# New written orders, buffers and warming places for a four-layer spectral kernel on one core

## The chip, the core and the metric

The kernel runs on one core of a Trainium2 chip. A core has a matrix engine (TensorE, PE in the profile, with PEld for its loading of weights), three engines that work on rows of up to 128 partitions (VectorE or DVE, ScalarE or ACT, GpSimd or POOL), and SyncE (SP), which here only issues transfers. The metric is the time of one execution on the device in microseconds (us).

## The reference

A sequence x of 2048 positions with 512 channels passes through four residual layers, A, B, A and B. A multiplies a two-dimensional spectrum by weights. B is a convolution along the sequence with a kernel K of its own for every channel, which is itself to be computed from the parameters; both B layers use the same K.

```python
def A(x):                                     # x: 1 x 2048 x 512
    return irfft2(rfft2(x) * (w_r + 1j * w_i), s=(2048, 512))

def B(u):                                     # 512 channels, 128 modes each
    dt = exp(log_dt)
    a = -exp(log_A_real) + 1j * A_imag
    C = (C_real + 1j * C_imag) * dt[:, None]
    P = exp((a * dt[:, None])[:, :, None] * arange(2048))
    K = 2.0 * einsum("dn,dnl->dl", C, P).real
    y = irfft(rfft(u.T, 4096) * rfft(K, 4096), 4096)[:, :2048]
    return y.T + u * D_skip

x = x + A(layernorm(x)); x = x + B(layernorm(x))
x = x + A(layernorm(x)); x = x + B(layernorm(x))
```

## The kernel before

**The work.** All Fourier transforms are matrix products with constant tables. The sequence is cut into 16 parts of 128 positions, so that a transform of 2048 is a pass over the 128 (products) and a pass over the 16 (products again, after a rearrangement). Data are tiles of 128 partitions by 512 numbers in f32.

- layer_a loads rows of x (`u`, line 428, on SP's queue; the table `ta` and the edge weights `ew` as well), takes layer-norm statistics (L359 to L382 on DVE), folds the rows (`spread`, L462 to L473), multiplies by tables on PE (halves, L330, and side_by_side, L336), by the spectral weights (L542 to L549 on DVE and POOL), and goes back.
- kernel_parts and kernel_time build K: exponentials and sines on ACT (L832), terms `qp` on DVE (L886, L888), products `pk` and their copies `kw` (L864), sums over the modes `pv` (L899), stored by way of `stage` (L907). kernel_constants (L812, L813) loads the tables `kb` and `ni` on POOL's queue; end_weights (L392 to L402) loads `ew` and prepares the end columns on POOL (L399).
- layer_b takes u's transform by row products into PSUM, copies them to `z` with ACT (L663), transposes z in 32 by 32 blocks on DVE (L669), multiplies by K's spectrum `kk` (`wb`, L991), adds (L1003, mostly POOL), transforms back (ACT copies in L1011 and L1015) and adds the residual (`za`, `xw`, L1029).

While the first A runs, K is computed; kernel_freq (K's spectrum) and the first B follow, with the rest of K between. Then come the second A and the second B, with nothing beside them. In the profiled execution the stages overlap. Roughly, the first A and most of K fill the first 300 us, the first B with the rest of K lies up to about 500, the second A up to about 613, and the second B, the last stage, from 613 to the end.

**The orders.** net_kernel emits all instructions in the order of the program. Then take_turns goes over each of the five engines: `TURNS[engine]` lists the engine's instructions by their number in emission, in the order in which they shall stand in the engine's stream. A list holds, for instance, 5046 numbers for PE. Each engine executes its own list strictly as a queue, except that waits between engines come from the data: an instruction waits until what it reads is written, and until the buffer that it writes is free. A transfer is issued by an instruction in a list too (mostly SP's), and the 16 DMA engines carry it out later.

**The buffers.** A phase is a group of pools in SBUF or PSUM, each with a tag, a size and a number of buffers ("rooms"). `ROOMS` says for each tile of a tag, in turn, which room it gets (room, L287).

**The pads.** Net.ps makes a tile in PSUM. `WARM` gives, for the number of a tile, how many pads are emitted ahead of its first product: a pad is one call of halves, two passes of 128x128 numbers of a constant tile `warm` against itself, written into the new tile and overwritten after. They keep PE busy where it would wait.

PE takes most products in two halves of 64 columns: halves emits one pass for each, with the output in the lower or upper 64 partitions of the PSUM tile; `128*64` in a row of the profile is such a half.

Of the kernel before, what the change touches and what calls it, by code (L numbers as in the profile page):

```python
# [10 lines left out]
F32 = mybir.dt.float32  # L11
# [27 lines left out]
WT = 4  # L39
WA = 7  # L40
# [16 lines left out]
MAG = 4  # L57
# [195 lines left out]
class Net:  # L253
# [870 lines left out]
def net_kernel(ctx, tc, x, w, ends, kin, log_dt, d_skip, out, **cst):  # L1124
# [19 lines left out]
    with ExitStack() as outer:  # L1144
        with ExitStack() as early:
            early.enter_context(net.phase("pk", P, pk=(2048, PK), pv=(2048, PV)))
            with net.phase("p", P, p1=(2048, 8 - PK - PV), p2="p1", p3="p1"), \
                    net.phase("a", x=(32768, 1), ta=(8192, 1), ca=(6912, 1), u=(16384, 2), w=(2056, WA), wt=(2056, WT),
# [4 lines left out]
                with net.phase("v", val=(10240, 1), hp=(HP, 2)):  # L1153
# [5 lines left out]
                    early.enter_context(net.phase("k", side="right", kw=(1024, 2), mag=(6144, MAG),  # L1159
# [10 lines left out]
            outer.enter_context(net.phase("b", t2=(8192, 1), u=(16384, 2), kk=(2048, 8), ta="t2", wt="w", wb="w", xw="w"))  # L1170
# [64 lines left out]
222-225 242-249 256-259 226-231 260 264-266 250 267 251 261 232 268-272 252 262 273 253 263 233 274-279 298-307  # L1235
280-281 254 312 282 286 255 313 287 314 288 315 289 283-285 308-311 316-321 290-291 322-331 338-339 292-295
340-342 346-349 343-345 296-297 350-351 332-335 366-371 358-365 336-337 374-387 414-417 372-373 402-413 418-423
464-465 424-427 388-393 448-451 466-467 452-455 476-483 512-513 456-461 514-515 394-397 516-517 398-401 462-463
428-431 518-519 432-433 520-523 434 436-437 435 438-439 352-357 548-551 554-557 524-525 468-475 552-553 440-441
484-487 558 492-494 504 495 559 505-507 488-491 442-447 496-497 526-533 498-499 508-511 500-503 534-543 560-561  # L1240
544-547 562-564 568 580 569 581 570 582 571 583 565-567 606-609 572-573 586-593 574-577 584 594 578 612 579 595
613 585 610 596-597 611 614-617 620-621 618-619 598-599 626-627 600-601 622-623 628 634-635 629-630 636-637
631-633 654-657 602-605 638-639 660-667 624-625 640-643 658 668-670 688 671 689 659 690-691 646-651 672-673
652-653 644-645 674-677 694-701 678 702-704 692 705 693 679 738-741 706-711 680-685 752-757 712 760 758 761 759
713 742-743 686 762-763 687 764-771 798-800 808-809 801-807 810-811 772-773 812 834-837 813-815 714-721 774-775
784-785 816-819 838-839 786-787 722-729 788-791 840-843 792-795 730-737 844-845 796-797 820-823 826-831 854-857
878 900-902 832-833 744-749 858-863 750-751 910 824-825 846-849 776-777 850-851 778-783 942 903 852-853 904-906
879-880 886-887 864-875 888 881-884 907-908 943-944 894-896 889-890 945 876-877 946-948 885 909 897 911-912
891-893 926-936 949 898 937-938 913-914 939 915-917 899 970-973 940-941 918-925 974-975 962-969 950-961 976-983
# [298 lines left out]
```

## Time and profile before

| | |
|---|---|
| time, three runs | 716.2, 717.33 and 723.59 us, median 717.33 |
| profiled execution | span 713.4 us; the page gives no other time of its own for it |
| instructions | 23503 |
| busy PE, DVE, ACT, POOL | 626.0, 601.9, 438.2, 357.3 us |
| moved by DMA | 81.32 MB, mean 114 GB/s |

The span is the time from the first to the last instruction of the profiled execution; a time of a run holds some microseconds around it. In a table of windows each row is one stretch in us from the span's start. It gives the busy time of each engine with its number of instructions, the granted clock of PE as a share of full speed (PEclk), and the mean busy share and rate of the DMA engines. A group row gives the line, engine, operation and tiles (written <- read), the number of instructions, their busy sum in us, the mean length of one in ns, and the idle time just before them with what ended it. A timeline row gives the start, the length, and in brackets the idle time before and who ended it.

### The profile page before, as it was taken

The page shows a single profiled execution, that of the slowest core. Times are in us where ns is not written, and L with a number is a line of the kernel's source. Part 1 is how long each engine was busy: PE and PEld are TensorE (multiplying, and loading weights), DVE is VectorE, ACT ScalarE, POOL GpSimd, SP SyncE. Part 2 cuts the span into 40 slices and gives each one's busy share as a digit, 9 for nine tenths or more (in the row PEclk, how much of TensorE's full clock was granted, in tenths as well). Part 3 has the DMA queues.
Part 4 walks back from the last instruction along what each step waited for, and adds up shares of the span by engine and source line. Part 5 has one row for each costly group of instructions (what it writes and reads, how often), then busy time and mean ns, then how long its engine had stood idle before and what let it go on. Part 6 is the DMA issues. An engine that isn't in the chain of part 4 may idle for free. (4 is left out here: it accounts for less than half of the span.)

```text
span 713.4 us, 23503 instructions
## 1 busy us (share of the span) xinstructions
PE 626.0 (88%) x9580; PEld 491.3 (69%) x9580; DVE 601.9 (84%) x1348; ACT 438.2 (61%) x946; POOL 357.3 (50%) x565
## 2 busy tenths in 40 slices
PE   4459989989996999889999997984989899999996
PEld 3237867878674867667858876774877766577876
DVE  4998497998999799969999676869588699799993
ACT  3558999997664796778868524333767427333322
POOL 1533528672852704543196356452056484286870
PEclk9779999999999999999999999997999999999999
DMA  8602611613558350455544689222123103335514
GB/s 282 229 0 89 210 48 47 122 62 43 167 133 245 107 138 32 65 128 94 163 62 136 195 198 246 80 106 75 61 77 89 46 2 104 125 103 149 156 34 111
DMA packets 137355, 81.32 MB, mean 114 GB/s; under 512 B 70976, under 2 KB 116928, under 8 KB 136352
## 3 DMA queue, kind: packets, MB, share of 16 engines
q1 hardware_dynamic: 136992, 79.30, 40.1%
q8 instruction: 76, 1.25, 0.7%
q0 software_dynamic: 256, 0.52, 0.4%
q14 instruction: 31, 0.25, 0.1%
HBM read 54.90 MB, written 25.43 MB: 113 GB/s over the span
## 5 line engine op out<-in xcount | busy, mean ns | idle before, releaser
L1003 POOL TENSOR_TENSOR u<-wb,wb 64x512 f32<-64x512 f32 x90 | 123.2, 1373 | 66.0 <-DVE wb L991 60.9
L336 PE MATMUL p<-z,mb 128*64 128x512 f32 (+2 forms) x480 | 108.0, 517 | 1.7 <-DVE wb L991 1.3
L899 PE MATMUL pv<-qp 128*64 128x128 f32 x1024 | 81.6, 279 | 5.0 <-ACT stage L907 4.2
L991 DVE TENSOR_TENSOR wb<-p,kk 128x512 f32<-128x512 f32 x128 | 81.5, 676 | 4.3 <-POOL u L1003 2.3
L336 PEld LDWEIGHTS p<-mb,u 128*64 128x64 f32 x2048 | 73.1, 138 | 13.1 <-issue 6.7
L336 PE MATMUL p<-mb,u 128*64 128x64 f32 x2048 | 74.3, 223 | 4.4 <-issue 2.0
L663 ACT COPY z<-p 128x512 f32<-128x512 f32 x96 | 52.4, 595 | 41.8 <-PE p L336 31.6
L669 DVE STREAM_TRANSPOSE z<-z 128x512 f32<-128x512 f32 x96 | 59.3, 675 | 19.8 <-ACT z L663 19.7
L899 PEld LDWEIGHTS pv<-qp 128*64 128x64 f32 x1024 | 64.4, 139 | 15.8 <-ACT stage L907 6.9
L1113 POOL TENSOR_SCALAR w<-w,norms 128x128 f32<-128x128 f32 x64 | 34.7, 554 | 67.7 <-DMA w<-h 29.8
L547 POOL TENSOR_TENSOR w<-w,w 64x257 f32<-64x257 f32 x48 | 34.7, 724 | 66.8 <-DVE w L542 45.3
L1015 ACT COPY u<-p 128x512 f32<-128x512 f32 x64 | 35.9, 590 | 48.7 <-PE p L336 45.3
L330 PE MATMUL p<-w,w 128*64 128x256 f32 x256 | 38.2, 438 | 27.8 <-DVE w L463 11.6
L330 PE MATMUL pk<-kb,th 96*64 96x256 bf16 (+1 forms) x384 | 56.5, 312 | 1.5 <-DVE qp L888 1.1
L542 DVE TENSOR_TENSOR w<-wt,p 128x514 f32<-128x514 f32 x64 | 42.7, 688 | 17.1 <-PE p L336 9.6
L864 DVE TENSOR_SCALAR kw<-pk 128x512 bf16<-128x512 f32 x64 | 42.9, 680 | 16.5 <-PE pk L330 16.1
L330 PE MATMUL p<-warm 128*64 128x128 f32 x612 | 49.2, 284 | 3.2 <-DVE half L1139 1.1
L336 PE MATMUL p<-t,w 64*64 64x128 f32 x1024 | 42.1, 280 | 10.2 <-DMA w<-kt 3.5
L336 PEld LDWEIGHTS p<-z,mb 128*64 128x64 f32 x480 | 39.7, 137 | 16.1 <-issue 7.9
L330 PEld LDWEIGHTS p<-w,w 128*64 128x64 f32 x256 | 24.7, 156 | 36.3 <-DVE w L463 12.7
L336 PE MATMUL p<-w,ca 128*64 128x257 f32 x256 | 45.0, 385 | 4.1 <-ACT w L526 1.5
L832 ACT ACTIVATE kf<-pk 128x512 f32<-128x512 f32 x64 | 38.8, 606 | 15.4 <-PE pk L330 13.8
(179 smaller groups left out, 1617.1 us busy)
## 6 DMA issues: line engine op xcount, KB each, us to landing
wt<-in_w SPq DMA_DIRECT2D x32, 257.0 KB, 2.7
kf<-kk SPq DMA_DIRECT2D x32, 256.0 KB, 3.3
kk<-kf SPq DMA_DIRECT2D x32, 256.0 KB, 2.7
u<-in_x SPq DMA_DIRECT2D x16, 256.0 KB, 6.8
hr<-in_x SPq DMA_DIRECT2D x16, 256.0 KB, 3.9
kt<-stage SPq DMA_DIRECT2D x32, 128.0 KB, 5.2
h<-hr SPq DMA_DIRECT2D x16, 256.0 KB, 3.0
w<-kt SPq DMA_DIRECT2D x32, 128.0 KB, 3.1
```

Source lines behind the costliest of these rows:

```text
L330: self.nc.tensor.matmul(out[64 * r:64 * r + 64], weights[:, 64 * r:64 * r + 64], data, **k)
L336: last = self.nc.tensor.matmul(out, weights, data, start=not more, stop=True, skip_group_check=True).ins
L542: nc.vector.tensor_mul(m[pl], W, px[:, None, :].to_broadcast([128, 2, 257]))
L547: e[0].tensor_sub(Y[0:64, v], m[0][hs, 0], m[1][hs, 1])
L663: nc.scalar.copy(tiles["z"][:, :, :, b, m:m + 2].rearrange("p u j m r -> p (u j) (m r)"), ps[b].rearrange("p u j m r -> p (u j) (m r)"))
L669: nc.vector.transpose(tiles["zt"][:, u:u + 8].rearrange("p u j d -> p (u j d)"), tiles["z"][:, u:u + 8].rearrange("p u j b m r -> p (u j b ...
L832: nc.scalar.activation(*a, **k)
L864: nc.vector.tensor_scalar(whole, p, MAGIC, -MAGIC, op0=ALU.add, op1=ALU.add)
L899: nc.tensor.matmul(p[64 * t:64 * t + 64, g], QP[:, c, 2, d:d + 2].rearrange("p s a -> p (s a)"), QP[:, c, 0:2, d:d + 2].rearrange("p k s b ...
L991: nc.vector.tensor_mul(split(m[c, pl], "du", [32, 16]), by_channel(p), split(k[c], "du", [32, 16]))
L1003: self.added = e[0].tensor_sub(y[0:64], v[0, 0], v[1, 1]), e[1].tensor_add(y[64:128], v[0, 1], v[1, 0])
L1015: nc.scalar.copy(V[:, :, j, :, d:d + 8].rearrange("p n q d -> p q n d"), p.rearrange("p (q n) d -> p q n d", q=2))
```

## The change

All instructions of real work stay as they are. Four things change.

1. phase() now also allocates every room of a tag at once when the phase opens, in a fixed order, and three phases (a, k and b) name their tags in another order. So tiles come to lie at other addresses.
2. The lists of TURNS are new for all five engines. PE's list has 4892 entries instead of 5046, by the pads; those of DVE (1348), ACT (922), POOL (561) and SP (316) are as long as before. Numbers in PE's list are those of emission with the pads counted, so the old and the new numbers of the same product differ.
3. WARM is new: 154 pads at 87 tiles instead of 231 at 92.
4. ROOMS is new: which room each tile gets.

Some moves that can be read from the lists: SP's rows of u come in the order 0, 1, 2, 3 instead of 0, 2, 1, 5, and the load of `ew` is ninth; POOL's issues of ni and kb are its 12th and 13th instruction instead of the first two, behind the first of end_weights (L399); ACT's early square root of one number (L1202, `root`) goes from first to about fifteenth.

The diff, with the lists cut to their first lines:

```diff
@@ -280,6 +280,11 @@
         with self.tc.tile_pool(name=name, bufs=1, space=space, side=side, reuse_waits="tile") as pool:
             for tag, v in tags.items():
                 self.tags[tag] = self.tags[v] if isinstance(v, str) else (pool, name, tag, *v)
+            for tag, v in tags.items():
+                if not isinstance(v, str):
+                    for k in range(v[1]):
+                        room = f"{tag}{k}" if v[1] > 1 else tag
+                        pool.tile([128, v[0] // 4], F32, tag=room, bufs=1, name=f"{name}_{room}")
             yield
         for tag in tags:
             del self.tags[tag]
...
@@ -1145,7 +1150,7 @@
         with ExitStack() as early:
             early.enter_context(net.phase("pk", P, pk=(2048, PK), pv=(2048, PV)))
             with net.phase("p", P, p1=(2048, 8 - PK - PV), p2="p1", p3="p1"), \
-                    net.phase("a", x=(32768, 1), ta=(8192, 1), ca=(6912, 1), u=(16384, 2), w=(2056, WA), wt=(2056, WT),
+                    net.phase("a", x=(32768, 1), u=(16384, 2), ta=(8192, 1), w=(2056, WA), ca=(6912, 1), wt=(2056, WT),
                               wv="w", junk="w"):
                 A = net.layer_a(w, src=xv, dst=hd)
                 early.enter_context(net.phase("k0", side="right", kb=(5120, 1), ni=(256, 1), th=(1536, TH)))
...
@@ -1156,7 +1161,7 @@
                         interleave(A[0][:PC])
                         interleave(A[0][PC:], made[:LATE])
                     net.end_weights(ends)
-                    early.enter_context(net.phase("k", side="right", kw=(1024, 2), mag=(6144, MAG),
+                    early.enter_context(net.phase("k", side="right", mag=(6144, MAG), kw=(1024, 2),
                                                   qp=(6144, QP), kf=(2048, KF), stage=(8192, 1)))
                     K, marks = net.kernel_time(parts, kt, list(range(32)), GROUP)
                     K = ahead(tc, K, KP)
...
@@ -1167,7 +1172,7 @@
                 with net.phase("e", hr=(2048, 8)):
                     interleave(K[cuts[0]:cuts[1]], A[2])
             outer.enter_context(net.phase("f", t=(16384, 1), z=(16384, 2), w=(2056, WB)))
-            outer.enter_context(net.phase("b", t2=(8192, 1), u=(16384, 2), kk=(2048, 8), ta="t2", wt="w", wb="w", xw="w"))
+            outer.enter_context(net.phase("b", kk=(2048, 8), t2=(8192, 1), u=(16384, 2), ta="t2", wt="w", wb="w", xw="w"))
             pm = [int(c) for c in PM.split(",")]
             early.enter_context(net.phase("pm", P, p1=(2048, pm[0]), p2=(2048, pm[1]) if pm[1] else "p1",
                                           p3=(2048, pm[2]) if pm[2] else "p1"))
...
     "tensor": """
-0-17 23-24 18-19 25-28 20-21 32-39 22 29-31 40-65 67-70 76-79 66 80-81 71-72 82-83 73-75 85-88 94-95 84 89-92
-103-106 93 96-97 112-113 107-108 98-101 109-110 102 114-115 111 116-119 121-124 120 125-126 130-131 127-128
-132-133 129 134-161 172-179 163-168 180-181 169-171 182-193 162 194-211 218-219 234-235 212-217 220-221 236-241
...
+0-1 9-10 18-27 11-16 2-5 28-29 17 6-7 30-31 8 32-33 35-38 34 39-65 76-77 67-68 66 69-74 78-81 75 82-83 85-88 84
+89-90 94-95 91-92 96-97 93 103-104 112-115 98-99 105-106 100-102 107-111 116-119 121-124 130-131 120 125-128
+132-135 129 136-153 157-158 154-155 168-169 156 170-171 159-160 166-167 161-162 172-173 176-177 163-165 178-189
+206-213 174-175 190-191 266-273 224-231 194-197 200-203 192-193 214 198-199 215-217 232 204-205 233-235 218-221
...
     "vector": """
-2 1 0 3-5 19 6 20 7 21 8 22 9 23 10-12 24 13-14 16-17 25 15 26 18 27-28 65 29 35 37 30 52 36 54 38 55 66 31 53
-39 41 76 101 40 78 32 77 42 79 43 59 67 80 82 119 81 83 121 123 60 125 84 44 72 85 102 68 61 73-74 33 75 86 34
...
+2 0 14 3 5 17 4 19 6 20 7 12 21 18 8 22 15 23 9 16 1 10 24 11 25 28 13 26 65 32 35 27 29 53 52 30 54 66 55 59 37
+39 36 101 38 41 76 40 42 78 43 48 80 77 82 60 119 31 72-73 79 121 81 67 44 122-123 83-84 61 68 125 120 85 126
+124 33 74 45 86 75 34 46 93 62 87 47 94 50 56 98 57 99 49 100 58 103 138 51 127 102 128 104 63 105 88-89 91 129
...
     "scalar": """
-611 0 9 1 5 2 6 23 10 24 11 14 34 15 3-4 7-8 12-13 29 50 18 51 40 39 49 16-17 19-20 25-26 52 30-31 35-36 64 62
...
+0 9 5 1 23-24 34 10-11 6 2 29 7 50 611 14 8 3 15 12 18 51 40 4 39 16 25 17 19 30 20 31 52 26 64 35-36 21-22 63
+62 61 13 41 27 42 32 28 49 33 45 53 57 54 37-38 58 46 73 43 69 44 78 70 65 47-48 66 83 55-56 98 59 79 74 60 67
...
     "gpsimd": """
-0-2 4 3 6 5 8 7 44-46 55 60 67 13 74 10 9 16-23 12 11 15 14 25 24 27 26 29 28 31 30 33 32 35 34 37 36 39 38 41
...
+3 5 10 2 6 8 7 9 44 4 45 1 0 24 46 14 11 13 15 25 12 16-19 28 20-21 67 22 74 32 27 30 33 29 23 26 60 31 54 35 34
+36 53 37 40 38 55 41 39 42 59 43 47-50 58 51 56 52 57 62-63 65 61 73 66 72 64 68 70 69 81 71 75 79 88 76-77 80
...
     "sync": """
-0 4 1 10 5 2 6 9 7 13 18 14 17 12 16 27 31 15 34 11 109 35 106 8 30 38 19 105 20 3 22 21 24 23 25-26 32-33
...
+0-1 4-5 7 2 6 9 27 12 10 13 11 17-18 8 15 30 16 14 19 31 20 35 38 34 105 3 22 21 106 23-24 26 25 28 33 29 32 37
+109 36 40-41 68 66 86 83 39 77 70 74 72 42 44 43 45 50-51 55 52 48 46 53 49 47 54 58 64 57 56 63 65 76 62 60 59
...
-WARM = {22: 7, 35: 3, 55: 1, 104: 3, 116: 2, 120: 5, 123: 6, 146: 2, 158: 1, 160: 2,
-        165: 2, 175: 3, 201: 1, 205: 2, 210: 2, 214: 2, 240: 2, 272: 1, 355: 1, 386: 1,
-        400: 1, 410: 1, 413: 1, 415: 4, 428: 1, 440: 5, 459: 1, 552: 3, 573: 3, 583: 1,
-        586: 1, 636: 1, 639: 3, 643: 2, 650: 2, 652: 7, 655: 4, 656: 3, 670: 1, 674: 1,
-        680: 5, 690: 3, 692: 2, 693: 1, 704: 1, 706: 3, 711: 1, 726: 1, 732: 1, 735: 3,
-        742: 1, 754: 5, 759: 3, 777: 1, 779: 2, 783: 2, 789: 4, 791: 1, 797: 3, 807: 1,
-        809: 1, 814: 3, 834: 1, 867: 1, 963: 3, 972: 4, 992: 1, 1007: 3, 1014: 6, 1017: 3,
-        1035: 1, 1105: 7, 1108: 1, 1111: 7, 1114: 3, 1121: 6, 1225: 2, 1226: 5, 1410: 1, 1443: 5,
-        1444: 2, 1530: 4, 1556: 1, 1572: 4, 1585: 2, 1587: 3, 1588: 2, 1589: 2, 1591: 2, 1595: 2,
-        1598: 1, 1611: 3}
+WARM = {35: 4, 55: 7, 127: 2, 165: 5, 284: 1, 362: 2, 518: 1, 538: 1, 557: 1, 596: 3, 613: 2,
+        618: 4, 641: 1, 711: 1, 714: 1, 753: 2, 754: 1, 757: 1, 777: 1, 800: 1, 807: 1, 809: 1,
+        818: 1, 834: 1, 861: 1, 879: 1, 893: 1, 909: 1, 912: 1, 942: 1, 947: 1, 950: 2, 980: 1,
+        1010: 1, 1105: 2, 1108: 1, 1111: 1, 1128: 5, 1130: 1, 1131: 3, 1142: 3, 1171: 1, 1178: 1,
+        1180: 1, 1184: 1, 1186: 1, 1194: 1, 1200: 1, 1203: 1, 1206: 1, 1208: 1, 1213: 1, 1219: 3,
+        1225: 3, 1228: 7, 1247: 2, 1249: 7, 1299: 2, 1305: 3, 1438: 1, 1572: 4, 1588: 7, 1595: 5,
+        1598: 1, 1622: 1, 1634: 1, 1635: 1, 1637: 1, 1649: 1, 1664: 1, 1680: 1, 1691: 1, 1693: 1,
+        1704: 1, 1716: 1, 1727: 1, 1739: 1, 1754: 1, 1760: 1, 1761: 1, 1772: 1, 1773: 1, 1774: 1,
+        1777: 1, 1785: 1, 1793: 1, 1804: 3}
 
 
 ROOMS = {
     "a.u": "0101",
-    "a.w": "0123456103254163052143651023456013250641253146025602513640213654120345612035164035204613025461324506"
...
...
-    "b.kk": "012345670123456701234567012345670123456701234567012345670123456701234567012345670123456701234567",
...
+    "a.w": "5243605102145304364102514631504126542134065142360132640125431236405136403210461325046352413602512326"
+        "50615464313060212463121404606535313402545063",
...
+    "b.kk": "214675030256314743517260306421045674526310472415265074160130165002314216503710570654623710256430",
...
```

More of the change, by code (lines that the diff above doesn't have):

```diff
@@ L1237 @@
[L1237 to L1246, printed above, removed]
@@ new lines @@
+    "v.hp": "101010",
+    "k0.th": "1010010101010110",
+    "k.mag": "01232103120312031230320103123201",
+    "pk.pk": "2101201201201201210102210210212012002110210210212011212012012012012002101201201221010102021021100122"
+        "0221021012012100102210210210",
+    "a.wt": "0321032102103021",
+    "k.kw": "1001101000101001110010011011001000110010001010101100101001110101",
+    "k.qp": "0102103223412304231024313241032141324013103241203102134221304213",
+    "e.hr": "2540136756012734",
+    "f.z": "0101010101010101001010101",
@@ new lines @@
+    "b.u": "100101",
+    "pb.p2": "122012012120120102212102",
+    "wide.wb": "61205742307542162160725451024156",
+    "pb.p1": "43203223410101320104323412001341304",
+    "wide.xw": "3021",
+    "pc.p3": "0120001200122202000000000120120121021202102102102101120122201200122012002210010201202112000121212120"
+        "1201112102010",
+    "folds.fa": "0101",
+    "folds.xf": "1010",
+    "pc.p1": "1001001101010101010010111010100110100110010101011010101001010110",
+    "pc.p2": "0221021012012012200121201021102010210210122121020102012021021012",
```

417 lines of the change are left out of this document (193 added, 224 removed).

## The prediction

> **What bounds the kernel now.** I read the head of the page first, then VectorE's (DVE's) waits, then the stages in a table of windows, and last the chain of work that ended last. The columns of a window row are busy us and count of PE, PEld, DVE, ACT and POOL, then PEclk, DMA share and GB/s.
>
> ```profile
> span 713.4 us, 23503 instructions
> PE 626.0 (88%) x9580; PEld 491.3 (69%) x9580; DVE 601.9 (84%) x1348; ACT 438.2 (61%) x946; POOL 357.3 (50%) x565
> PEclk9779999999999999999999999997999999999999
> ```
>
> Two engines are nearly full, TensorE (PE) with 626.0 us and DVE with 601.9. The span is 87 us above the one and 111 above the other, so neither alone is the limit: they take turns, and an order can win only what lies in the change of turns. The table of windows shows who leads where.
>
> ```profile
> 20.00:40.00 20.00, 5.17 (x38) 2.96 (x34) 19.98 (x37) 11.92 (x18) 13.34 (x20) 0.64 0.48 169
> 40.00:60.00 20.00, 16.09 (x116) 11.07 (x118) 19.68 (x60) 12.55 (x34) 5.13 (x13) 0.84 0.03 8
> 60.00:80.00 20.00, 20.00 (x241) 17.81 (x236) 10.06 (x20) 18.75 (x40) 7.40 (x20) 1.00 0.48 148
> 180.00:300.00 120.00, 111.10 (x1508) 80.46 (x1506) 114.23 (x302) 83.36 (x160) 62.15 (x94) 0.99 0.49 131
> 613.00:669.00 56.00, 54.18 (x1019) 39.48 (x1017) 54.25 (x88) 19.10 (x39) 40.76 (x30) 1.00 0.41 120
> 669.00:700.00 31.00, 30.20 (x660) 25.75 (x657) 28.25 (x47) 10.46 (x23) 20.76 (x16) 1.00 0.34 96
> ```
>
> From 20 to 60 DVE is full (19.98 and 19.68 of 20). From 60 PE is full and DVE half empty. From 180 to 300 DVE leads, with 5.8 us free in 120. From 613 to 700 both are full, and there any work added on either costs time. What DVE waits for elsewhere stands in its list of waits (us in total, times, longest):
>
> ```profile
> DVE z L669 <- ACT z L663: 19.7, 6, 6.2
> DVE kw L864 <- PE pk L330: 16.1, 8, 7.5
> DVE za L1029 <- PE p L336: 13.3, 6, 6.0
> DVE w L542 <- PE p L336: 9.6, 6, 7.8
> DVE bst L359 <- DMA u<-in_x: 8.1, 2, 5.7
> ```
>
> These five make 66.8 of DVE's 111 idle us. The first four end behind PE (ACT's z copy of L663 waits for row products too), so what PE does ahead of those products sets them.
>
> **The change part by part.** All counts of orders and pads come from the two sets of lists; their times are those of the row of before in which the same work runs. Apart from the pads the instructions are the same ones; ScalarE's new order, in which the root of L1202 goes from first to about fifteenth, implies one activation-table load fewer (24 to 23), near the start where ACT is half empty. About four in five instructions of each engine stand at another position, but by 13 places on PE and 4 on DVE in the mean: the stages remain, and their insides are permuted. The new allocations in phase() and the order of its tags change addresses, for which I count nothing. ROOMS decides who waits for a buffer; no row prices that, so it goes into the range through the rivals.
>
> **Pads.** WARM goes from 231 pads to 154, each two passes: 924 passes become 616.
>
> ```profile
> L330 PE MATMUL p<-warm 128*64 128x128 f32 x612 | 49.2, 284 | 3.2 <-DVE half L1139 1.1 <-DVE w L542 1.0 <-ACT w L526 0.7
> L330 PE MATMUL pk<-warm 128*64 128x128 f32 x276 | 21.5, 276 | 0.8 <-DVE qp L888 0.8
> L330 PE MATMUL pv<-warm 128*64 128x128 f32 x36 | 3.2, 281 | 0.1
> 75.36 1.42 PE L330 MATMUL pk<-warm 128*64 128x128 f32 x22
> ```
>
> The mean of 284 ns is a latency; in a run of 22 they take 1.42 us, so one costs (1.42-0.27)/21 = 0.055 us, with 0.27 for the last one's latency (row 53.86 below). 308 fewer are 17 us of PE time. What that is worth depends on the stage:
> - 57 to 80: 64 passes become 8, 3.1 us less. PE leads there, but a pad mostly stands where PE waits for another engine anyway (ACT has 18.75 of 20). I take **1.0 us**, between 0 and 3.1.
> - 180 to 300: 316 become 100, 11.9 us less on PE. DVE leads, so this is worth only what DVE waits for: of its 5.8 free us, 4.01 stand in one place (row 243.99), before transposes that wait for ACT copies of row products. The PE work ahead of those products, the trace's own durations summed in the two orders, falls by about 11 us, so the gap mostly goes: **2.7**, between 0 and 5.8.
> - 613 to the end: 12 become 124, 6.2 us more. Here PE has 1.8 us free up to 669 and 0.8 up to 700, which can hide 2.6. I charge **3.0**, between 0 and 6.2.
> - The rest: 140 become 32 from 80 to 180 and 124 become 68 from 510 to 613, 9 us less on PE; DVE's order around its gaps there is unchanged, so I count nothing.
>
> ```profile
> 243.99 2.49 DVE L669 STREAM_TRANSPOSE z<-z 128x512 f32<-128x512 f32 x4 [4.01 <-ACT z L663]
> 320.90 0.69 DVE L864 TENSOR_SCALAR kw<-pk 128x512 bf16<-128x512 f32 x1 [6.54 <-PE pk L330]
> 414.92 4.86 DVE L669 STREAM_TRANSPOSE z<-z 128x512 f32<-128x512 f32 x8 [6.18 <-ACT z L663]
> 439.69 4.86 DVE L669 STREAM_TRANSPOSE z<-z 128x512 f32<-128x512 f32 x8 [4.21 <-ACT z L663]
> ```
>
> **Gaps of DVE in the middle.** At 320.90 DVE waits 6.54 us for a kernel product. The new order puts seven transposes ahead of this kw, and 19 row products that feed them ahead on PE. At 4.86/8 = 0.61 us each the seven are 4.3 us, work that now fills the gap if its copies are ready. Twelve small instructions at 338 move before another gap of 1.21. I take **3.5**, between 0 and 7.7. At 414.92 and 439.69 DVE's own list is only permuted among the eight transposes of one tile, so it helps only as PE brings the products earlier; PE's work ahead of them falls by about 20 us, most of which is work moved behind, and 100 pad passes fewer from 360 to 440 are 5.5. I take **3.0** of the 10.4 us in these two rows. At 72, 476, 507, 565, 608 and 700, DVE's other long waits, its order is unchanged around the gap, and I take nothing there. From 440 to 510, 28 passes become 132 in a stretch where PE idles and the clock falls (last row below): if the clock holds, 10.58 us of PE work at 0.74 lose 2.7 less; I take **1.0**.
>
> ```profile
> 480.00:500.00 20.00, 10.58 (x142) 9.12 (x144) 18.30 (x75) 8.40 (x29) 5.46 (x6) 0.74 0.21 68
> ```
>
> **The start.** SP loads rows of u and POOL's queue loads kb (L812) and ni at once. DVE waits:
>
> ```profile
> 1.27 0.73 POOL L812 DMA_DIRECT2D kb<-in_kb  x1 [0.82 <-POOLq L1538]
> 10.13 1.29 DVE L359 BATCH_NORM_STATS2 bst<-u 128x6 f32<-128x512 f32 x2 [5.67 <-DMA u<-in_x]
> 6.00:8.00 2.00, 0.00 (x0) 0.00 (x0) 0.00 (x0) 0.00 (x0) 0.00 (x0) 1.00 0.99 239
> 10.00:12.00 2.00, 0.00 (x0) 0.00 (x0) 1.87 (x6) 0.20 (x1) 0.90 (x3) 1.00 1.03 414
> q0 software_dynamic: 256, 0.52, 22.6%
> kb<-in_kb POOLq DMA_DIRECT2D x1, 480.0 KB, 8.6
> 70.70 0.52 PE L330 MATMUL pk<-kb,th 96*64 96x512 bf16 x2
> ```
>
> From 6 to 8 the DMA engines are full but move 239 GB/s, against 414 from 10 to 12, after kb has landed. The fifth row is POOL's queue in the first 14 us: 22.6% of the engines' time, 3.2 us of each. The new order of POOL issues kb and ni only behind L399, which waits for ew, and the new order of SP moves that load to ninth place and brings the rows in the order 0, 1, 2, 3 rather than 0, 2, 1, 5. I credit 3.2 us for kb and 1.3 for the order of rows, a row of 256 KB at some 200 GB/s: **4.5**, between 0 and the gap's 5.7. DVE leads from there to 60, so the gain stays. If kb came late, PE's first pk product would wait; issued at 20 even, and with its 8.6 us to landing, it is there 40 us before its first use at 70.70. POOL's instructions behind L399 wait with it for ew; POOL has 13.34 of 20 from 20 to 40, so I count nothing.
>
> **Neighbours on one half of PE.** Most products use 64 columns of the array, and the written order mostly alternates halves. Consecutive products on the same half rise from 262 to 462. Does a pass wait behind its neighbour's half?
>
> ```profile
> 681.48 0.28 PE L336 MATMUL p<-mb,u 128*64 128x64 f32 x2
> 681.60 0.59 PE L336 MATMUL p<-z,mb 128*64 128x512 f32 x1
> 681.68 0.28 PE L336 MATMUL p<-mb,u 128*64 128x64 f32 x2
> 53.86 0.27 PE L473 MATMUL p<-w,edge 128*64 128x128 f32 x1
> 53.97 0.27 PE L473 MATMUL p<-w,edge 128*64 128x128 f32 x1
> ```
>
> The z product at 681.60 starts before the pair at 681.68 that stands ahead of it in before's order: the halves run on independently, some passes deep. So only long one-sided runs cost; I charge **2.0** for 200 more neighbours. If each cost its pass, the two rows at 53.86 and 53.97, neighbours on one half, put it at 0.11 us, 22 us in all.
>
> [...]
>
> **The sum.** -4.5 -1.0 -2.7 -3.5 -3.0 -1.0 +3.0 +2.0 = -10.7. The span of 713.4 becomes 702.7. The three times shown are 716.2 to 723.59 with a median of 717.33, and the page gives no time of its own for the profiled execution, so around the span lie 2.8 to 3.9 us: 705.5 to 706.6, and I take **706**.
>
> **The rivals.**
> A, slower: PE's halves hold each other up. [...] For it: 89 of the 200 new neighbours stand between 510 and 700, where PE is full. Against it: row 681.60. Price: 200 at 0.11, of which 43 fall under DVE's cover from 180 to 240 (4.7 us), is 17.3; the 28 from 613 on cost more if they are 512-column passes (the one at 681.60 lasts 0.59 against 0.28 for narrow ones), 0.3 more each, 8.4. Less the 2 charged already, +23.7: span 726.4, time about **730**. It decides from 0.06 us a neighbour on, where 200 of them eat the 10.7.
>
> B, no change: DVE's gaps come back one product later, since most of their instructions stay where they are, or the clock falls where pads went. The start's 4.5 stays, the last stage's pads and halves cost 5, the middle gives 0 to -2: span 712 to 714, time about **716**. For it: the list of waits, where four of five wait for PE products that other waits set. Against: 216 fewer passes in 180 to 300. The clock's share is bounded:
>
> ```profile
> 220.00:240.00 20.00, 16.52 (x270) 13.56 (x268) 19.87 (x82) 10.00 (x19) 5.82 (x9) 0.91 0.81 247
> 260.00:280.00 20.00, 7.70 (x100) 5.59 (x100) 0.00 (x0) 1.00 0.22 79
> 260.00:280.00 20.00, 20.00 (x320) 15.82 (x320) 19.74 (x52) 18.06 (x36) 5.12 (x8) 1.00 0.22 79
> ```
>
> The middle row holds the pads alone (PE, PEld and DVE): without them PE has 12.3 us of 20 there, and at 0.64, the lowest clock of the table, 19.2: still covered. [...]
>
> C, faster still: the middle gaps close to their bounds, 5.8, 7.7 and 7.5 instead of 2.7, 3.5 and 3.0, 11.8 more: span 690.9, time **694**. For it: DVE's own list keeps little ahead of those gaps. Against: the work that fills them has to be ready.
>
> That the change does not do what it says is a part of this: the real work is the same, but 154 tensor instructions are gone.
>
> **How the numbers follow.** Forecast (700 to 711, its own range) 0.48, C 0.09, B 0.28, A 0.15. About 1% is what a measurement of this kernel can tell from no change: faster is below 710.2, slower above 724.5. Forecast and C give faster 0.56 (0.01 of the forecast's range lies above the line), B same 0.29, A slower 0.15. The range leaves out the lower half of C and the upper two thirds of A, 0.15: **692 to 726**.
>
> **What would show it.** Right at the start: the second stats at L359 near 6, not 10.13, and kb issued after L399. In the middle: L669's waits for ACT under 10 us in total (19.7 now), kw's under 10 (16.1). PE near 610 busy with 616 warm passes. The clock at 1.00 in what is now 480 to 500. In the last stage, as long as before plus 3 to 5. A would show PE full but stages from 510 longer, with products waiting for nothing; B the same sums of waits under other names. Wrong altogether: a wait on a buffer of the new ROOMS at the head of DVE's list, which nothing here prices.

## The result, and the profile after

The changed kernel takes 749.18 us in the median (748.37 to 752.76), before 717.33: 1.048 times before, with a 95% interval of 1.0439 to 1.0521. 706 was forecast, in a range of 692 to 726. It is slower by more than rival A allowed (730). The head of the page after:

```profile
span 747.5 us, 22798 instructions
PE 683.0 (91%) x9272; PEld 486.3 (65%) x9272; DVE 602.4 (81%) x1348; ACT 437.5 (59%) x945; POOL 351.0 (47%) x565
PEclk9699999999985999999999999998999999999999
```

The other engines did the same work in about the same time (ACT with 23 table loads instead of 24, of 1.28 us each). PE has 308 matmul passes fewer and is busy 57 us **longer** (683.0 against 626.0). The clock explains only a small part: its longest stretch at 0.50 that before does not have, 24 us from 218 to 242, is at most 12 us of work. That is an estimate, half of the 24: two pk passes of 512 columns take 0.64 us at 240.84, in that stretch, and 0.38 at 242.60, behind it. The groups of the same products, before and after, with only their line numbers moved by 5 (columns: count, busy sum in us, mean of one in ns, idle before them):

```profile
L336 PE MATMUL p<-z,mb 128*64 128x512 f32 (+2 forms) x480 | 108.0, 517 | 1.7 <-DVE wb L991 1.3 <-DVE z L669 0.3
L336 PE MATMUL p<-t,w 64*64 64x128 f32 x1024 | 42.1, 280 | 10.2 <-DMA w<-kt 3.5 <-ACT z L663 2.8 <-DMA t<-in_t 2.4
```

```profile
L341 PE MATMUL p<-z,mb 128*64 128x512 f32 (+2 forms) x480 | 148.4, 521 | 1.8 <-DVE wb L996 1.7
L341 PE MATMUL p<-t,w 64*64 64x128 f32 x1024 | 65.6, 302 | 3.4 <-DMA w<-kt 2.2 <-POOL w L1118 0.9 <-ACT z L668 0.3
L341 PEld LDWEIGHTS p<-t,w 64*64 64x64 f32 x1024 | 40.6, 142 | 35.9 <-issue 28.7 <-DMA t<-in_t 2.4 <-ACT z L668 1.9
```

One pass lasts nearly as long as before (517 and 521 ns; 280 and 302). The sums grew by 40 and 24 us mostly because the passes overlap less. Note the two shapes: z,mb uses 128 rows of the array (128\*64), t,w only 64 (64\*64). In before the 1024 passes of t,w, of 280 ns each, fit into 42.1 us, nearly seven in flight at a time; of z,mb it was little over two. DVE's waits, the list that the prediction began with, and after it two rows of before's list:

```profile
DVE wb L996 <- PE p L341: 25.3, 25, 2.8
DVE z L674 <- ACT z L668: 23.6, 8, 10.9
DVE kw L869 <- PE pk L335: 23.1, 17, 7.0
DVE za L1034 <- PE p L341: 13.7, 9, 6.0
DVE kf L967 <- ACT kk L959: 10.0, 3, 7.0
```

```profile
DVE wb L991 <- PE p L336: 1.2, 2, 0.9
DVE kf L962 <- ACT kk L954: 0.9, 1, 0.9
```

Of the five waits that the prediction listed, three are longer (z, kw and za), w's is 8.2 us instead of 9.6, and that of the first statistics for rows is 1.3 instead of 8.1. Two are as good as new: 25 waits of wb for PE products, 18.8 of its 25.3 us after 613, and kf's for ACT's copies of K's spectrum (kk), 10.0 us, nearly all of it between 415 and 426.

Where the time went shows when one asks at which time PE had finished as many real products as before had at t. Delays in us against before, counted from the traces, good to about half a microsecond (e5, e9 and e13 are experiments below):

| t in before | 60 | 180 | 220 | 260 | 300 | 360 | 500 | 610 | 640 | 680 |
|---|---|---|---|---|---|---|---|---|---|---|
| after | -7.7 | -11.0 | -8.9 | -0.2 | 4.7 | 7.0 | 13.9 | 11.8 | 23.8 | 32.4 |
| e5 | -8.3 | -11.6 | -9.6 | -7.0 | -0.9 | 0.8 | 2.6 | 0.0 | 8.7 | 13.5 |
| e9 | 0.3 | 0.2 | -0.2 | 0.3 | 2.1 | 2.0 | 1.8 | 0.6 | 10.4 | 19.0 |
| e13 | -7.1 | -10.4 | -8.4 | -3.8 | 2.2 | 3.9 | 5.3 | 5.9 | 9.3 | 8.3 |

Up to 180 us the change is a gain of 11. From 220 to 500 it loses 23, and in the last stage 20 more. All of these are stages with products of K's spectrum and of layer B, in which both shapes occur.

### The profile page after: what moved, and what is told of

Read it like the earlier page. It is cut to its first block, busy times and chain, and to the rows that moved or that the text cites. A ratio compares the mean times of both kernels' runs of the same rounds, so it can differ in the third digit from the quotient of the medians.

```text
span 747.5 us, 22798 instructions
## 1 busy us (share of the span) xinstructions
PE 683.0 (91%) x9272; PEld 486.3 (65%) x9272; DVE 602.4 (81%) x1348; ACT 437.5 (59%) x945; POOL 351.0 (47%) x565
## 4 chain that ended last, share of the span: by engine, by line
PE 66%; DVE 14%; ACT 9%; DMA 6%; issue 4%; POOL 1%; SPq 1%; DVEq 0%; ACTq 0%; POOLq 0%
PE p L341 39%; PE p L335 16%; PE pv L904 6%; PE pk L335 4%; DMA wt<-in_w 2%; DVE qp L893 2%; DVE w L547 1%; DMA w<-kt 1%; DVE bst L364 1%; DVE qp L891 1%; DVE kw L869 1%; DMA u<-in_x 1%; ACT z L668 1%; ACT hp L804 1%; ACT w L531 1%
## 5 line engine op out<-in xcount | busy, mean ns | idle before, releaser
L341 PE MATMUL p<-z,mb 128*64 128x512 f32 (+2 forms) x480 | 148.4, 521 | 1.8 <-DVE wb L996 1.7
L996 DVE TENSOR_TENSOR wb<-p,kk 128x512 f32<-128x512 f32 x128 | 83.5, 682 | 30.8 <-PE p L341 25.3
L904 PE MATMUL pv<-qp 128*64 128x128 f32 x1024 | 100.2, 285 | 3.9 <-ACT stage L912 3.1
L904 PEld LDWEIGHTS pv<-qp 128*64 128x64 f32 x1024 | 71.6, 140 | 24.1 <-issue 12.4
L674 DVE STREAM_TRANSPOSE z<-z 128x512 f32<-128x512 f32 x96 | 59.5, 677 | 23.8 <-ACT z L668 23.6
L341 PE MATMUL p<-t,w 64*64 64x128 f32 x1024 | 65.6, 302 | 3.4 <-DMA w<-kt 2.2
L341 PEld LDWEIGHTS p<-mb,u 128*64 128x64 f32 x2048 | 65.4, 138 | 3.2 <-issue 2.8
L335 PE MATMUL pk<-kb,th 96*64 96x256 bf16 (+1 forms) x384 | 62.8, 320 | 3.0 <-DVE wb L998 1.1
L341 PEld LDWEIGHTS p<-t,w 64*64 64x64 f32 x1024 | 40.6, 142 | 35.9 <-issue 28.7
L335 PEld LDWEIGHTS p<-warm 128*64 128x64 f32 x548 | 45.3, 148 | 25.6 <-issue 19.2
L335 PE MATMUL p<-warm 128*64 128x128 f32 x548 | 58.4, 294 | 1.8 <-ACT x L480 1.0
L341 PEld LDWEIGHTS p<-z,mb 128*64 128x64 f32 x480 | 41.0, 136 | 22.8 <-issue 14.6
L335 PE MATMUL p<-ca,u 128*64 128x128 f32 (+2 forms) x512 | 52.3, 302 | 1.7 <-ACT u L568 1.7
```

Source lines behind the costliest of these rows:

```text
L335: self.nc.tensor.matmul(out[64 * r:64 * r + 64], weights[:, 64 * r:64 * r + 64], data, **k)
L341: last = self.nc.tensor.matmul(out, weights, data, start=not more, stop=True, skip_group_check=True).ins
L674: nc.vector.transpose(tiles["zt"][:, u:u + 8].rearrange("p u j d -> p (u j d)"), tiles["z"][:, u:u + 8].rearrange("p u j b m r -> p (u j b ...
L904: nc.tensor.matmul(p[64 * t:64 * t + 64, g], QP[:, c, 2, d:d + 2].rearrange("p s a -> p (s a)"), QP[:, c, 0:2, d:d + 2].rearrange("p k s b ...
L996: nc.vector.tensor_mul(split(m[c, pl], "du", [32, 16]), by_channel(p), split(k[c], "du", [32, 16]))
```

## The experiments

**The first four: halves, clock, start.** I began with rival A (neighbours on one half of the array), the clock, and the credit for the start. In e1 some products change places so that halves alternate, for instance:

```diff
 "tensor": ... (after)
-192 193 214 198 199 215 216 217 232
+192 193 198 214 215 199 216 217 232
```

> The changed kernel with PE's list alone touched: 1272 of its 4892 products and pads stand up to 11 places elsewhere (0.5 in the mean), so that neighbours alternate between the halves of the array more often (242 neighbours on one half instead of 462; 262 in before). Everything else is as changed. Theory 1 (halves): a product does not start before the one ahead of it in PE's list, so neighbours on one half leave the other half idle; summing the traces' pass lengths by that rule gives 560.3 us of PE stream for before, 588.9 for the changed kernel and 564.5 here. In the stages where PE leads (300 to 360, and from 613 on) 11 us go, so the time falls by 9 to 14, to 735 to 740. Theory 2 (clock): nothing changes there, the time stays within 3 us of 749. Theory 3 (the other engines' orders and the buffers make new waits): PE has room, so nothing changes beyond 3 us.

Measured: 782.35 us, 1.0886 times before (1.0819 to 1.0953). Neighbours on one half were fewer than in before, and the time rose by 33 us. Theory 1 as it stood cannot be right; theory 3 has a part, since some products now stand ahead of others that were ready. DVE's and ACT's lists and the buffers were not touched. In the measure of the table above, e1 stands at -3.3 at 180 us where the changed kernel stands at -11.0. The strict queue that theory 1 starts from, and that the text on the orders gives for every engine, is not quite PE's: at 52 of before's 5045 pairs of neighbours in the list, 681.60 among them, the second product's first pass starts ahead of the first product's, and at 167 of 4891 after. In both traces DVE's 1348, ACT's 922 and POOL's 561 instructions do start in the order of their lists.

e2 gives the PSUM tiles whose products lie from 180 to 300 us the pads of before, 79 instead of 25:

```diff
-WARM = {..., 518: 1, 538: 1, 557: 1, 596: 3, 613: 2, 618: 4, 641: 1, ...}    # after: 154 pads
+WARM = {..., 552: 3, 573: 3, ..., 650: 2, 652: 7, 655: 4, 656: 3, ...}       # 208 pads
```

> The changed kernel with before's pads for the PSUM tiles whose products lie from 180 to 300 us in before (158 passes instead of 50 there), each ahead of its tile's first product. Everything else is as changed. Theory 2 (clock): the granted clock, 0.50 from 218 to 242 in the changed kernel, returns to 1.00 after at most 4 us, PE does in that stretch what took 24 us in about 14, and the time falls by 8 to 10, to 739 to 741. Theory 1 (halves): 108 passes more at 0.055 are 6 us of PE, partly covered by DVE: the time rises by 0 to 5. Theory 3: no change, 749.

Measured: 754.11 (1.0519, 1.0453 to 1.0585). The two windows, after first:

```profile
220.00:240.00 20.00, 19.70 (x173) 12.17 (x174) 9.46 (x40) 8.55 (x15) 6.69 (x11) 0.50 0.49 140
```

```profile
220.00:240.00 20.00, 18.76 (x269) 12.91 (x268) 13.45 (x54) 11.47 (x22) 8.52 (x14) 1.00 0.54 160
```

With the pads the clock did not fall (1.00 instead of 0.50), but of the 96 passes more in the window 64 are pads. The 4 us at 0.50 that were expected at most are near what before has in this window: 0.50 for 3.4 us, from 230.5 to 233.9, and 1.00 from 234 to 240. By 260 the kernel is 1.8 us ahead of the changed one (-2.0 against -0.2 in the measure of the table above), by 300 it is 3.7 behind (8.4 against 4.7). What the clock gives the pads take, as far as this run tells. Theory 2 does not carry the loss.

e3 changes only the start of before:

```diff
 "sync":    -0 4 1 10 5 2 6 9 7 13 ...      +0 1 4 5 2 6 9 27 10 7 13 ...
 "gpsimd":  -0 1 2 4 3 6 5 8 7 44 45 46     +2 4 3 6 5 8 7 44 45 1 0 46
```

> Before with two edits of the start alone: SP issues rows 0, 1, 2, 3 of u first, then ta, kin, one more row and ew, and POOL issues ni and kb behind L400 (the second instruction of end_weights) instead of first. If the load of kb held up the rows (the prediction's step for the start, 4.5 us): DVE's stats start by 6 us instead of 10.1 and the time falls by 4 to 6, to 711 to 713. If the gain at the start of the changed kernel (8 us by 60 us) came from the other engines' orders instead: less than 2 us.

Measured: 719.56 against 718.2, 1.0012 (0.9974 to 1.0049): nothing. DVE's timeline in e3, and the sums of six windows from 0 to 60 us, before, e3 and after:

```profile
5.70 0.69 DVE L359 BATCH_NORM_STATS2 bst<-u 128x6 f32<-128x512 f32 x1 [0.64 <-DMA u<-in_x]
...
23.49 1.88 DVE L359 BATCH_NORM_STATS2 bst<-u 128x6 f32<-128x512 f32 x3 [2.52 <-DMA u<-in_x]
```

```profile
sum 60.00, PE 30.73 PEld 21.06 DVE 49.60 ACT 30.20 POOL 21.60; mean PE 5.12 PEld 3.51 DVE 8.27 ACT 5.03 POOL 3.60
```

```profile
sum 60.00, PE 30.58 PEld 20.71 DVE 49.67 ACT 30.30 POOL 21.26; mean PE 5.10 PEld 3.45 DVE 8.28 ACT 5.05 POOL 3.54
```

The load did move: the second stats start at 5.70 instead of 10.13. But DVE's written order then runs into rows that land later (23.49), and by 60 us it has done 49.67 us of work, as before. In the changed kernel, with another list, it has done 51.87; that the list makes the difference was not tested by itself.

e4 does the opposite of e1, on before, in the last stage:

```diff
 "tensor": ... (before)
-4117-4121 4150 4152 4151 4153
+4117 4118 4120 4119 4121 4150 4152 4151 4153
```

> Before with PE's list alone touched, in the last stage (products of 613 to 700 us): 358 places are permuted by at most 3, so that neighbours stand on the same half of the array more often (504 in all instead of 262). No pads are moved or added. Theory 1 (halves): the PE stream grows by 19.4 us, all in a stage where PE leads, and the time by 14 to 20, to 731 to 737, with the 512-column products of the stage costing most. Theory 3, or halves that run on independently as the prediction had it: PE looks some products ahead, permuting by at most 3 places costs under 3 us, 716 to 720.

Measured: 739.03, 1.0304 (1.0242 to 1.0367): 358 small moves cost 21 us, about what theory 1 said (14 to 20). But e4 also mixed the two shapes, which I had not counted.

**What the four have in common.** PE's busy time in the last stage without pads was 85.0 us in before, 104.2 after, 104.7 in e1 and 106.6 in e4. Neighbours of 128 rows on one half number 40, 49, 26 and 242 there; changes between a product of 64 rows and one of 128 rows, in either direction, 23, 67, 77 and 69. Only the second count goes with the time. What such a change does can be seen in PE's timeline, after first, then before:

```profile
669.25 0.97 PE L341 MATMUL p<-z,mb 128*64 128x480 f32 x2
670.15 0.45 PE L341 MATMUL p<-t,x 64*64 64x128 f32 x8
670.53 1.14 PE L341 MATMUL p<-z,mb 128*64 128x512 f32 x6
...
672.53 1.02 PE L341 MATMUL p<-z,mb 128*64 128x512 f32 x2
673.48 0.43 PE L341 MATMUL p<-t,x 64*64 64x128 f32 x4
673.85 1.07 PE L341 MATMUL p<-z,mb 128*64 128x512 f32 x2
```

```profile
660.28 1.10 PE L336 MATMUL p<-t,x 64*64 64x128 f32 x32
661.32 0.64 PE L336 MATMUL p<-z,mb 128*64 128x512 f32 x1
```

The z products of 669.25 run until 670.22, and the t,x products begin at 670.15; those of 672.53 end at 673.55, t,x begins at 673.48. Each time PE is nearly empty (0.07 us) before a product of the other row height starts. In before 32 passes of t,x stand together in 1.10 us and pay that once on each side; after, 12 passes pay it four times. Over the whole list there are 92 such changes in before and 268 after, and these rows are no exception: at not one of them does the next product start more than 0.09 us before the end of everything ahead of it in the list, while at 4827 of before's 4953 other pairs of neighbours it does. (Starts are recorded; the ends are modelled by the profile.)

**e5: only the shapes.** Products of 64 rows that start close to one another are put together, 628 places in all; nothing else:

```diff
 "tensor": ... (after)
-1270 1271 1134 1272 1273 1135-1138 1141 1139 1143 1140 1340 1341 1142
+1270-1273 1134-1138 1141 1139 1143 1140 1142 1145 1144
```

> The changed kernel with PE's list alone touched: 628 products stand a few places elsewhere, so that products of 64 rows (64*64 in the trace: t,x and t,w) stand together. Changes between products of 64 rows and of 128 rows fall from 268 to 152 (before has 92); neighbours on one half of the array stay at 429 (462 in the changed kernel). Theory 4 (switches), formed from the four kernels so far: the array empties at each such change. PE's busy time in the last stage without pads is 85.0 us in before, 104.2 in the changed kernel, 104.7 in e1 and 106.6 in e4, with 23, 67, 77 and 69 changes and 40, 49, 26 and 242 neighbours on one half: 0.4 us for a change, 0 to 0.2 for a neighbour fit all four. By it 116 changes fewer are up to 46 us of PE, and the time falls by 15 to 35, to 715 to 735. Theory 1 (halves): no change, 745 to 752.

Measured: 731.48, 1.0208 (1.0148 to 1.0269), 18 us less than the changed kernel.

```profile
PE 655.1 (90%) x9272; PEld 483.7 (66%) x9272; DVE 600.9 (82%) x1348; ACT 436.2 (60%) x945; POOL 352.4 (48%) x565
...
L341 PE MATMUL p<-t,w 64*64 64x128 f32 x1024 | 51.7, 289 | 4.9 <-DMA w<-kt 2.8 <-ACT z L668 2.1
```

PE's busy time falls by 27.9 us for 116 changes, at most 0.24 us each, since the clock has a part in it (0.74 from 220 to 240 instead of 0.50, by estimate up to 0.24 of the 20 us, so 5); t,w goes from 65.6 to 51.7. Neighbours on one half stayed (431, 462 in the changed kernel), as the edit meant.

**e6: shapes and halves** (the same rule, and among products of one shape the one on the other half first; 1479 places, of the kind of e1's).

> As e5 (152 changes between 64 and 128 rows instead of 268), and neighbours alternate between halves besides (182 on one half instead of 462); 1479 products stand elsewhere. Theory 4 (switches): as e5, 715 to 735, within 5 us of it. Theory 1 (halves): 10 to 20 us below e5.

Measured: 755.33 (1.0547, 1.0473 to 1.0620), 24 us **above** e5. PE's busy time is 659.0 in e6 and 655.1 in e5, so alternating halves brought nothing on PE, and the time went into waits: PE stands idle for 90 us of the span instead of 74. One that grew, by 8.2 us, is DVE's for ACT's w, from e6 and from e5:

```profile
DVE w L602 <- ACT w L599: 13.1, 17, 3.6
```

```profile
DVE w L602 <- ACT w L599: 4.9, 4, 3.6
```

The reading that fits: two tiles whose products are interleaved are both finished late, and who reads the first one waits. Part of e1's loss must be of this kind: by 180 us, ahead of the first product of 64 rows, it is already 7.7 us behind the changed kernel.

**e7 and e8: the price by itself.** Both add 30 pads to before's last stage, at the same places; those of e8 multiply 64 rows:

```diff
-            self.halves(t[:, 0:128], self.warm[:, 0:128], self.warm[:, 64:192], start=True, stop=True)
+            (self.quads if self.n in {...} else self.halves)(t[:, 0:128], self.warm[:, 0:128], self.warm[:, 64:192], start=True, stop=True)
...
+        for r in range(2):
+            self.nc.tensor.matmul(out[64 * r:64 * r + 64], weights[0:64, 64 * r:64 * r + 64], data[0:64], **k)
```

> Before with 30 more pads in its last stage, one ahead of the first product of each of 30 tiles, where only products of 128 rows stand around them. The pads are the usual ones: 120 passes of 128 rows. It is the control for e8. Both theories: 120 passes at 0.055 are 6.6 us, 2.6 of it in PE's free time: 2 to 7 us more, 719 to 724.

> As e7, but each of the 30 pads multiplies 64 rows instead of 128 (same count of passes, same columns, same places). Theory 4 (switches): 60 changes between 64 and 128 rows more, at 0.4 us up to 24 us: 12 to 24 us above e7. Theory 1 (halves): the same neighbours as e7, the same time within 3 us.

Measured: e7 723.10 (1.0071, 1.0032 to 1.0111), e8 732.40 (1.0215, 1.0160 to 1.0270). 60 changes cost 9.3 us, 0.16 each, below what I expected (12 to 24). PE's timeline in e8 and in e7:

```profile
645.25 0.80 PE L342 MATMUL p<-mb,u 128*64 128x64 f32 x20
645.98 0.43 PE L336 MATMUL p<-warm 64*64 64x128 f32 x4
646.35 0.34 PE L342 MATMUL p<-mb,u 128*64 128x64 f32 x4
646.61 0.44 PE L336 MATMUL p<-warm 64*64 64x128 f32 x4
646.98 0.45 PE L342 MATMUL p<-mb,u 128*64 128x64 f32 x6
```

```profile
632.22 0.57 PE L336 MATMUL p<-mb,u 128*64 128x64 f32 x12
632.62 0.39 PE L330 MATMUL p<-warm 128*64 128x128 f32 x4
632.84 0.63 PE L336 MATMUL p<-mb,u 128*64 128x64 f32 x16
```

From a pad to the next products passes 0.37 us in e8 (645.98 to 646.35) and 0.22 in e7 (632.62 to 632.84). Around the pads stand mostly narrow products of 64 columns, which end soon (0.22 us); between z products of 512 columns (0.59) there is more to wait for. That fits 0.16 here, at most 0.24 over all of e5 and about 0.4 in the last stage, but the width was not tested by itself.

**e9 and e11: the last stage.** e9 gives before the changed kernel's last stage: the second layer B's part of all five lists, of ROOMS and of WARM. e11 takes the 38 pads of that stage out of the changed kernel.

```diff
 e9   "vector": ... (before; one stretch, the other lists, ROOMS and WARM likewise)
-1208 1209 1219 1220 1212 1211 1210 1221 1222 1213
+1208 1209 1211 1212 1210 1221 1222 1219 1220 1213
 e11  WARM: the entries of the second layer B's tiles are left out (154 pads become 116)
```

> Before with the changed kernel's last stage alone (the second layer B): orders of all engines, buffers and pads of that stage from the changed kernel, everything ahead as in before. 36 changes between products of 64 and of 128 rows more (128 instead of 92), 21 pads more. Theory 4 (switches): 36 at 0.4 are 14 us, 84 passes of pads 4.6, of which 2.6 find PE free: 12 to 20 us more, 730 to 738. If the last stage of the changed kernel is slow for what comes ahead of it (data or buffers late): within 3 us of before.

> The changed kernel without the 38 pads of its last stage (152 passes); nothing else is touched. Cost of the pads there: 152 at 0.055 are 8.4 us if PE is full all the way, as it is with 20.00 of 20 from 660 to 720. Theory 4 and theory 1 alike: 5 to 8 us less, 741 to 745. If pads only fill time in which PE waits: no change, 748 to 750.

Measured: e9 736.84 (1.0266, 1.0224 to 1.0308), 18 us more, so the last stage carries its loss with it wherever it stands. Of the 18 us, 84 passes more of pads are 4.6 at 0.055 each; the rest is 0.38 for each of 36 changes, if the other lists and buffers of the stage cost nothing. e11 742.67 (1.0347, 1.0289 to 1.0405), 6.5 us less: the pads cost most of what their 152 passes take (8.4).

**e10, e12, e13, e15: can it be repaired?** e12 groups e5's list once more by e5's own times (112 changes); e10 adds before's last stage to e12; e13 adds it to e5; e15 puts before's pads from 180 to 300 into e13.

```diff
 "vector": ... (e13, from after; the second layer B's part only)
-1208 1209 1211 1212 1210 1221 1222 1219 1220 1213
+1208 1209 1219 1220 1212 1211 1210 1221 1222 1213
```

> As e5, with PE's list regrouped once more by e5's own times: 112 changes between 64 and 128 rows instead of e5's 152, 907 products stand elsewhere than in e5. Theory 4 (switches): 40 at 0.4 are up to 16 us of PE: 715 to 728 (e5: 731.5). If moving products so far makes their readers wait, as e6 suggests (its waits of DVE for ACT rose): 731 to 745.

> The changed kernel with PE's list regrouped as in e5, once more with e5's own times (products that start within 1 us of each other may change places), and with before's last stage (all engines, buffers, pads). 114 changes between 64 and 128 rows instead of 268. Theory 4 (switches): e5 stood 1 us behind before where the last stage begins; with 38 changes fewer it is 5 to 15 us ahead there, and the last stage costs what it costs in before: 703 to 715. If the changed kernel's other orders lose elsewhere what its start wins: 716 to 724.

> e5 (the changed kernel with 152 changes between 64 and 128 rows instead of 268) with before's last stage besides (all engines, buffers and pads of the second layer B): 142 changes. e5 measured 731.5, and the changed last stage cost 18 in e9. If the two add up: 713 to 720, no longer slower than before. If regrouping had already taken the last stage's part: 722 to 730.

> As e13, with before's pads from 180 to 300 us instead of the changed kernel's (33 pads more). Clock: e5 still fell to 0.53 from 220 to 230; if that costs, the pads bring 2 to 6 us, 709 to 716. If the pads only take PE's time, as in e2: 0 to 5 us more than e13.

Measured: e12 745.00 (1.0405, 1.0347 to 1.0464) and e10 731.42 (1.0194, 1.0142 to 1.0246), both above what the count of changes says. PE's busy time in e12 is 651.2, 4 us below e5, yet the kernel takes 13.5 us longer, and PE is idle for 91 us of the span instead of 74. That products moved by up to 1 us of time make others wait, as in e6, fits this; it was not followed to single waits. e13 takes 721.78 (1.0051, 1.0020 to 1.0082), half a per cent above before: regrouping and the old last stage give back about 27 of the 32 us. e15 takes 730.98 (1.0172, 1.0129 to 1.0214), 9 us more than e13. Against e13 these are 54 pads (the 33 expected are counted against the changed kernel), 216 passes or 11.9 us at 0.055: again the pads take PE's time. But e15 does not test the clock, since with the pads it was no higher (0.57 against 0.60). From 220 to 240, e13 first:

```profile
220.00:240.00 20.00, 18.35 (x194) 12.87 (x194) 10.42 (x43) 9.32 (x18) 6.67 (x11) 0.60 0.56 163
```

```profile
220.00:240.00 20.00, 18.07 (x172) 12.78 (x172) 10.63 (x46) 5.85 (x11) 6.11 (x9) 0.57 0.34 94
```

None of these beats before, though e13 is still 10 us ahead at 180.

## Why the prediction was wrong

The step that failed is the one that is not in the sum: PE's order was taken as harmless ("their insides are permuted") apart from halves. The sum has no term for changes between products of 64 and of 128 rows. There are 176 more of them, and at the 0.16 to 0.4 us that e8, e5 and the last stage show they are, by estimate, 28 to 70 us of PE; the busy time without pads rose by about 74 (57 us, and 17 for the pads that went), up to 12 of it by the clock, by the estimate above. e5 and e13 show what that is worth in time: 18 us back by regrouping alone, 27 with before's last stage. The row at 660 us shown above, with 32 passes of one shape together, was in the profile before.

- **Start, -4.5:** gain right and larger (-7.7 by 60 us), mechanism wrong. kb's load was in the way of the rows, but e3 shows that moving loads alone gains nothing. What is left are the new lists of the engines, which no run changes by themselves.
- **Pads 57 to 80, -1.0:** from 60 to 180 the gain grows by 3.3 us, about half of it by 80. So the size fits, but orders and 108 passes from 80 to 180, for which nothing was counted, changed as well.
- **180 to 300 and the gaps up to 480, -9.2 in all:** wrong in sign. Of the four gaps only kw's behaved as forecast: 6.54 us became 2.19, with 2.04 ahead of the transposes now in front of it. The first grew from 4.01 to 10.9 us, in part by the clock (6.6 in e2, where it was 1.00), and in front of the transposes of 414.92, where DVE's list was taken as hardly changed, two kf now stand that were ahead of that stretch before, and wait 7.0 and 2.3 us for ACT. From 220 to 500 the changed kernel loses 22.8 us and e5 12.2, so the shapes that e5 grouped are about half of it; e5 has some 100 changes left there, before 54. (Rival C closed the last two gaps by 7.5 us; their rows hold 10.4, and no row gives the 7.5.)
- **Clock, -1.0:** not gained. From 480 to 500 it is 1.00, as forecast, but the low stretch only came later (0.93 from 440 to 510 before, 0.93 from 450 to 520 after). And it fell where pads went, from 218 to 242, as rival B feared; in e2, with its pads, it stayed at 1.00 at no profit, in e15, with pads too, it was 0.57. B's bound took 0.64, a mean over 20 us, as the lowest clock; but before has 0.50 from 230.5 to 233.9, and at 0.50 B's 12.3 us of work in 20 would be, by estimate, up to 24.6, which DVE does not cover.
- **Pads in the last stage, +3.0:** right in kind, too small. e11 takes out 152 passes for 6.5 us, so the 112 that the term counts are about 4.8, inside its range. PE has almost no free time left there, as the window of most of that stage shows (PE 58.59 of 59):

```profile
631.00:690.00 59.00, 58.59 (x872) 34.36 (x872) 42.35 (x70) 17.26 (x34) 33.05 (x25) 1.00 0.28 83
```

- **Halves, +2.0:** right to be small. e6 has 183 such neighbours instead of e5's 431 and PE's busy time does not fall. So rival A came true in sign and, for the last stage, in place, by another mechanism. Its price per neighbour is not borne out: e5 has nearly as many such neighbours as the changed kernel and is 18 us faster, and e6 has few and is slower than e5.
- A slip without effect on the sum: a pad is two products and four recorded passes, not two; 924 and 616 are records (and in e2's expectation 158 and 50 are products, so its 6 us of PE should be 12). After, 548, 36 and 32:

```profile
L335 PE MATMUL p<-warm 128*64 128x128 f32 x548 | 58.4, 294 | 1.8 <-ACT x L480 1.0 <-DVE w L547 0.4 <-ACT u L1016 0.4
L335 PE MATMUL pk<-warm 128*64 128x128 f32 x36 | 6.6, 278 | 0.0
L335 PE MATMUL pv<-warm 128*64 128x128 f32 x32 | 4.2, 279 | 0.0
```

Open: what remains between 220 and 500 us in e13 (some 14 us from -8.4 to 5.3). It has more changes there than before (some 100 against 54). The clock is 0.60 from 220 to 240, where before has 0.91, which is by estimate up to 0.31 of the 20 us, so 6, and kf's wait for ACT, new with the changed lists, is 9.9 us in e13 too. Buffers, pads and the other engines' lists differ as well, and these were not told apart.

## What to carry to other kernels

When instructions of PE are put in another order, count the changes of tile shape between neighbours first (0.16 to 0.4 us each here, between 64 and 128 rows): a search whose model does not price them will scatter small products among large ones. Keep products of one shape together, but only by moving those that are ready at the same time: the kernels that moved more of them (e6, e12) lost it again in idle time of PE. A load that comes earlier need not be worth anything: in e3 it came 4 us earlier, and the engine that reads it, in its old order, waited further on.

## What was not expected of the hardware

A change between products of 64 and of 128 rows all but empties PE (0.07 us of overlap): 0.16 us each among narrow products (e8 against e7), about 0.4 in the last stage. Alternating the halves of 64 columns brought nothing on PE (659.0 us busy in e6, 655.1 in e5). And the clock stayed at 0.50 from 220 to 240 while the records show PE busy for 19.70 of 20 us, in 173 passes; in e2, with 269 passes, it was 1.00. That pair alone does not show that more passes raise it, since in e2 the clock had not fallen before: from 210 to 220 PE was busy for 8.10 us there and for 6.57 in the changed kernel. But e15 has pads in the window and 172 passes, and its clock is 0.57. So a window that the profile calls busy, with ends of passes that it models, can have a low clock: 0.50 with PE busy for 19.70 of 20 us, 0.57 with 18.07 in e15. What sets the clock was not tested by itself.
